# Values, zeros of the order table and gate weights loaded behind the keys and queries of the first quads

## The chip, the cores and the metric

The kernel runs on one NeuronCore of one Trainium2 chip. The metric is device time in microseconds (us). The time before is 711.22 us, the median of three runs.

The engines are named as the profile names them: PE is TensorE's matmuls and PEld its weight loads, DVE is VectorE, ACT is ScalarE, POOL is GpSimd, and SP is SyncE, which here only issues transfers (DMAs). Each engine works through its own instructions in a fixed order; between engines and transfers there are semaphores to wait for. A transfer that SP issues is spread over the core's 16 DMA engines, and the transfers of its queue are served in the order of issue.

## What is computed

```
attention, for 8 batches x 8 heads, 576 tokens, 64 dims, 32 landmarks:
    q_lm, k_lm = means of q and k over groups of 18 tokens
    A = softmax(q k_lm'),  Bm = softmax(q_lm k_lm'),  C = softmax(q_lm k')
    Z = inverse of Bm by 6 Newton steps
    x = A Z C v                                   # 4608 tokens x 512
experts:
    logits = x w_gate;  e = argmax(logits);  gate = softmax(logits)[e]
    out = gate * (relu(x w1[e]) w2[e])            # 8 experts, 512 -> 1024 -> 512
```

All arrays are float32 in HBM. q, k and v are 9.4 MB each.

## The kernel before

**Quads.** The attention works on quads, four heads of one batch: quad i is batch i // 2, heads 0 to 3 or 4 to 7; there are 16. For each quad `load` (line 105) issues one transfer of 576 KB each for keys (`ld_k`), queries (`ld_q`) and values (`ld_v`). They go into a pool with two buffers of each name, so the keys of quad i + 2 wait until quad i's have been read. Below, k0, q0 and v0 stand for keys, queries and values of quad 0, and so on.

**Stages.** `period(i)` (line 408) lets the stages of several quads run side by side. Quad i is in `front`: TensorE transposes its keys and queries head by head (`transposed`, line 112, three transposes of a head into one of two PSUM buffers), ScalarE copies them out, GpSimd (keys, lines 131 to 136) and VectorE (queries, line 125) make the sums for the landmarks. Quad i - 1 is in `middle`: the means (line 141), the products (line 169), and two softmaxes (VectorE's maximum, line 184 to 187; ScalarE's exponential `ce`, line 190). Quad i - 2 is in `values`: transposes of `ce` (line 253), products with the values (line 259), and products with the gate's weights `wg` (line 273). Later stages invert, multiply, and write the tokens to DRAM; from the logits each token's number and gate are scattered into the DRAM table `order` (line 558), which has to hold zeros before.

**Order.** `merge` runs the stages' generators side by side, and a scheduler sets each engine's order from the order and priority in which the code is traced, and from times that it assumes. `period(i)` issues keys and queries of quad i + 1 (for i = 0 also those of quad 0), then the values of quad i - 1. The transfer of `wg` is issued in the constructor of `Attention` (line 98), and the one that writes zeros into `order` (288 KB, line 479) in that of `Routing`, from a tile `zero` that also feeds 14 products that nothing reads (line 478), put there for TensorE's clock.

**Experts.** After the attention the tokens, sorted by expert, go in slots of 128 through the two products of their expert (line 814). This loop has all of its weights and rows in time and is the longest part of the program.

Of the kernel before, what the change touches and what calls it, by code (L numbers as in the profile page):

```python
# [22 lines left out]
M = 32                  # landmarks  # L23
P96, J = 96, 6          # token s = 6 p + j
NT = B * S
DM, NE, DF = 512, 8, 1024
QUAD = 264              # [4 heads x 64 | 8 gate logits]
ITER = 6
BOOST = {0: 0, 1: 0, 2: 0, 3: 200, 5: 200}      # of the stages, by their lag
LAST = 1 << 20  # L30
XG = 4                  # buffers of gathered rows
# [7 lines left out]
def merge(tc, *streams):  # L39
    """Runs generators (generator, units, boost) side by side, each at an even pace; the scheduler prefers the boosted."""  # L40
# [18 lines left out]
class Attention:  # L59
    """Tokens into DRAM, in rows [4, 4, 32]: column (q, c, i) is number 128 c + 32 q + i."""  # L60

    def __init__(self, tc, ctx, front, psum, q, k, v, wg):
# [15 lines left out]
        self.ending, self.pair, self.rows = False, 0, []  # L78
# [7 lines left out]
        e2 = c.tile([128, 2, D], F32, name="e2")            # sums the two halves and takes the mean  # L86
# [11 lines left out]
        nc.sync.dma_start(out=self.wg, in_=wg.rearrange("(h d) e -> d h e", d=D))  # L98
        self.src, self.quads, self.cs, self.ats, self.bs, self.z, self.done, self.fin, self.two = ({} for _ in range(9))

    @staticmethod
    def at_col(j):
        """Where the columns (j % 2, j // 2, p) hold the tokens of j."""
        return 288 * (j % 2) + 96 * (j // 2)

    def load(self, i, names):
        b, g = divmod(i, 2)
        for n in names:
            t = self.src[i, n] = self.ld.tile([P96, 4, J * D], F32, name=f"ld_{n}")
            self.nc.sync.dma_start(out=t, in_=getattr(self, n)[b, 4 * g:4 * g + 4].rearrange("h (p j) d -> p h (j d)", j=J))  # L110

    def transposed(self, i, name):
        """Four heads, [128 (j % 2, d), 4, 288 (j // 2, p)], and their landmarks in both halves [128, 4, 32]."""
# [32 lines left out]
    def front(self, i):  # L146
        """Transposes of quad i; of the last batch also what its inverse needs."""
# [29 lines left out]
    def softmaxes(self, i, outer=None, inner=None):  # L177
        """Of ql . k and ql . kl, without their divisions by the sums."""
# [21 lines left out]
    def middle(self, i):  # L200
        """The softmaxes of quad i."""
# [13 lines left out]
        # softmax over the landmarks of q . kl  # L215
# [23 lines left out]
    def values(self, i):  # L239
        """C v of quad i, and its products with the gate's weights."""  # L240
# [38 lines left out]
    def chain(self, b):  # L279
        """Transposes of the inverses Z of batch b, in blocks.  # L280

        Newton's steps 2 Z - Z B Z from Z = c B' give c B' P, P = (I + R)(I + R^2)...(I + R^32), R = I - c B B'."""
# [6 lines left out]
        bt = self.bk.tile([128, 2, W], F32, name="bt")          # transposed: blocks on the diagonal, and side by side  # L289
# [15 lines left out]
        cc = self.sm.tile([128, 2], F32, name="cc")             # - c  # L305
# [16 lines left out]
        rp = self.bk.tile([128, 2, W], F32, name="rp")          # R^(2^k) in blocks, P  # L322
# [26 lines left out]
    def apply(self, b):  # L349
        """Z C v and Z C v w_gate of batch b, in blocks."""  # L350
# [21 lines left out]
    def final(self, b):  # L372
        """The tokens of batch b."""
# [34 lines left out]
    def period(self, i, nb, extra=()):  # L408
        """One quad's time: quad i is transposed, others are in later stages."""
# [3 lines left out]
        if i + 1 < n:  # L413
            self.load(i + 1, "kq")
        if 0 <= i - 1 < n:
            self.load(i - 1, "v")
# [28 lines left out]
SLOTS = NT // 128 + NE - 1     # at most; NT // 128 at least  # L445
EARLY = 2                       # slots that the most frequent expert of the first CHOOSE batches fills for sure
# [4 lines left out]
class Routing:  # L451
    """The tokens' numbers and gates in DRAM, sorted by expert, NT places for each."""

    def __init__(self, tc, ctx, front, psum, order):
# [19 lines left out]
        # products that nothing reads release TensorE's clock before the first loads arrive  # L474
# [4 lines left out]
        nc.sync.dma_start(out=order.rearrange("(p a) o -> p (a o)", p=128), in_=zero)  # L479
# [552 lines left out]
```

## Time and profile before

| | |
|---|---|
| median of three runs | 711.22 us (709.11 to 712.07) |
| span of the profiled execution | 707.1 us |
| time of the profiled execution outside its span | not given; the median is 4.1 us above the span |
| busy in the span | PE 659.2 us (93%), DVE 521.8 (74%), ACT 400.6 (57%), POOL 343.4 (49%) |
| DMA | 84.70 MB, 120 GB/s on average |

The busy times are averages over stages with different limits. The page divides the span into 40 slices of 17.7 us; one line of it gives the clock that TensorE was granted in each, in tenths. Its two levels are 1.2 and 2.4 GHz, and a slice between 5 and 10 tenths had both. The timelines give each engine's work in order of time, with the idle time before a piece and what ended it in brackets.

### The profile page before, as it was taken

The numbers are of one execution on the slowest core, as the hardware profiler recorded it, in microseconds if no ns is written. First come the engines' busy times: TensorE is split into PE (matmuls) and PEld (weight loads), VectorE is DVE, ScalarE is ACT, GpSimd is POOL, SyncE is SP. The second block draws the span as 40 slices with busy tenths as digits, with TensorE's granted clock in tenths as the row PEclk, the third lists the DMA queues.
The fourth block names the chain that finished last, engine by engine and source line by source line (L and its number), as shares of the span: only waits on it lengthen the run. The fifth ranks groups of instructions, "written<-read, shape, count | busy, mean of one in ns | idle before, by whom it ended". The sixth has DMA issues, their size and how long they took to land.

```text
span 707.1 us, 13813 instructions
## 1 busy us (share of the span) xinstructions
PE 659.2 (93%) x4489; PEld 517.5 (73%) x4489; DVE 521.8 (74%) x1409; ACT 400.6 (57%) x997; POOL 343.4 (49%) x371
## 2 busy tenths in 40 slices
PE   7798989898889869889999999999999999999996
PEld 4576767676667546667888888888888888888884
DVE  2389858579697976657879879876689879857653
ACT  3377656556566563335666666654477576544442
POOL 3355564556447154577654544544445454351231
PEclk8589998978897998999999999999999999999999
DMA  9877676668843171128224514411143333410010
GB/s 201 186 197 176 188 150 167 126 172 177 210 112 98 45 211 35 47 64 300 69 70 142 176 53 160 162 45 57 50 142 110 119 116 112 144 57 35 31 49 29
DMA packets 45386, 84.70 MB, mean 120 GB/s; under 512 B 7954, under 2 KB 26388, under 8 KB 45280
## 3 DMA queue, kind: packets, MB, share of 16 engines
q1 hardware_dynamic: 35232, 63.24, 33.4%
q0 software_dynamic: 10048, 20.29, 9.0%
q8 instruction: 38, 0.62, 0.4%
q14 instruction: 68, 0.56, 0.3%
HBM read 64.29 MB, written 19.73 MB: 119 GB/s over the span
## 4 chain that ended last, share of the span: by engine, by line
PE 46%; DMA 4%; issue 3%; DVE 1%; POOL 1%; ACT 0%; POOLq 0%; DVEq 0%
PE ps_tp L814 12%; PE ps_fi L814 12%; PE ps_ch L814 12%; PE ps_fr L814 11%; DMA xg<-xs,read 4%; DVE h L834 0%; POOL out_dram L845 0%; POOL xg L782 0%; DVE buf L795 0%; DVE ht_lo L800 0%; ACT ht_hi L797 0%; POOLq L880 0%; POOLq L845 0%; DVEq L795 0%; DVEq L771 0%
## 5 line engine op out<-in xcount | busy, mean ns | idle before, releaser
L845 POOL DMA_INDIRECT out_dram<-buf,write x38 | 39.0, 1026 | 166.2 <-ACTq L771 140.6
L782 POOL DMA_INDIRECT xe<-xs,read x84 | 87.7, 1044 | 25.7 <-issue 24.1
L782 POOL DMA_INDIRECT xg<-xs,read x80 | 83.0, 1038 | 30.5 <-issue 23.0
L797 ACT CAST ht_hi<-buf 128x512 fp32r<-128x512 f32 x76 | 47.1, 622 | 71.3 <-DVE buf L795 70.4
L834 DVE TENSOR_SCALAR h<-ps_tp 32x256 f32<-32x256 f32 x152 | 64.1, 422 | 26.9 <-PE ps_tp L814 24.6
L834 DVE TENSOR_SCALAR h<-ps_fi 32x256 f32<-32x256 f32 x144 | 60.7, 422 | 28.5 <-PE ps_fi L814 26.1
L832 ACT ACTIVATE h<-ps_tp 32x256 f32<-32x256 f32 x152 | 57.3, 377 | 41.2 <-PE ps_tp L814 37.4
L832 ACT ACTIVATE h<-ps_fi 32x256 f32<-32x256 f32 x144 | 54.2, 377 | 34.5 <-PE ps_fi L814 30.7
L814 PE MATMUL ps_ch<-whi,ht_hi 128*128 128x512 f32 x152 | 59.7, 393 | 1.0 <-ACTq L771 1.0
L814 PE MATMUL ps_fr<-whi,ht_hi 128*128 128x512 f32 x152 | 60.4, 398 | 0.0
L814 PE MATMUL ps_fr<-wlo,ht_hi 128*128 128x512 f32 x152 | 60.0, 395 | 0.0
L814 PE MATMUL ps_fr<-whi,ht_lo 128*128 128x512 f32 x152 | 59.8, 393 | 0.0
L558 POOL DMA_INDIRECT order<-i_tok,l_at x48 | 44.8, 932 | 30.5 <-issue 9.6
L814 PE MATMUL ps_ch<-wlo,ht_hi 128*128 128x512 f32 x152 | 59.4, 391 | 0.0
L814 PE MATMUL ps_ch<-whi,ht_lo 128*128 128x512 f32 x152 | 59.2, 389 | 0.0
L392 PE MATMUL ps_fi<-w,at 128*96 128x264 f32 x160 | 51.2, 415 | 7.9 <-DVE l L396 5.1
L795 DVE STREAM_TRANSPOSE buf<-h 128x512 f32<-128x512 f32 x76 | 49.7, 692 | 5.8 <-DMA out_dram<-buf,write 2.0
L800 DVE TENSOR_TENSOR ht_lo<-buf,ht_hi 128x512 fp32r<-128x512 f32 x76 | 51.1, 692 | 3.8 <-ACT ht_hi L797 0.2
L759 DVE TENSOR_TENSOR wlo<-raw,whi 128x512 fp32r<-128x512 f32 (+1 forms) x64 | 48.9, 820 | 4.2 <-ACT whi L758 4.1
L814 PE MATMUL ps_tp<-whi,xt_hi 128*128 128x512 f32 x152 | 49.4, 405 | 2.2 <-ACTq L771 2.2
L814 PE MATMUL ps_tp<-whi,xt_lo 128*128 128x512 f32 x152 | 48.5, 401 | 0.0
L814 PE MATMUL ps_tp<-wlo,xt_hi 128*128 128x512 f32 x152 | 48.1, 398 | 0.0
(275 smaller groups left out, 1572.3 us busy)
## 6 DMA issues: line engine op xcount, KB each, us to landing
raw<-in_moe_w_dram SPq DMA_DIRECT2D x48, 512.0 KB, 6.1
ld_k<-in_k_dram SPq DMA_DIRECT2D x16, 576.0 KB, 5.4
ld_q<-in_q_dram SPq DMA_DIRECT2D x16, 576.0 KB, 11.8
ld_v<-in_v_dram SPq DMA_DIRECT2D x16, 576.0 KB, 7.6
xs<-xrow SPq DMA_DIRECT2D x44, 192.0 KB, 4.6
xe<-xs,read POOLq DMA_INDIRECT x84, 2.5
xg<-xs,read POOLq DMA_INDIRECT x80, 3.0
order<-i_tok,l_at POOLq DMA_INDIRECT x48, 6.0
```

Of the source, the lines that this page charges most:

```text
L392: nc.tensor.matmul(po[g][:P96, :QUAD], lhsT=ats[g][:, n:n + 96], rhs=w[:, g, :], start=True, stop=True)
L558: self.nc.gpsimd.indirect_dma_start(out=self.places[n + j], out_offset=bass.IndirectOffsetOnAxis(ap=at[:, j:j + 1], axis=0), in_=self.tok[ ...
L759: (engine or nc.vector).tensor_tensor(out=l, in0=x, in1=h.bitcast(F32), op=ALU.subtract)
L782: self.nc.gpsimd.indirect_dma_start(out=x[:, t, :], out_offset=None, in_=src.rearrange("n (q c) -> (n q) c", q=4), in_offset=bass.Indirect ...
L795: nc.vector.transpose(out=x.rearrange("p c (t j) -> p t c j", t=4), in_=src[:, :, 32 * c:32 * c + 128].rearrange("p t (c i) -> p t c i", c=4))
L797: nc.scalar.copy(out=hi[:, c:c + 4, :], in_=x)
L800: nc.vector.tensor_tensor(out=lo[:, c:c + 4, :], in0=x, in1=hi[:, c:c + 4, :].bitcast(F32), op=ALU.subtract)
L814: nc.tensor.matmul(ps[c // 512] if type(ps) is list else ps[:, c // 512], lhsT=x0[:, a, :], rhs=w[:, a, c:c + 512], start=a == 0 and j == ...
L832: nc.scalar.activation(out=dst, in_=src, func=AF.Relu)
L834: nc.vector.tensor_scalar(out=dst, in0=src, scalar1=0.0, scalar2=None, op0=ALU.max)
L845: nc.gpsimd.indirect_dma_start(out=self.outs[s], out_offset=bass.IndirectOffsetOnAxis(ap=at, axis=0), in_=y, in_offset=None, bounds_check= ...
```

## The change

The loads of `wg` and of the zeros leave the constructors. `wg` is issued in `period(1)`, v0 in `period(1)` and v1 in `period(2)`, each ordered behind the last load of queries issued so far; the zeros are written after `period(2)`, ordered behind v1. Loads of quads 0 and 1 (keys, queries and values) are made as two transfers of two heads each. The tile `zero` and its 14 products stay. (The full diff also strips comments, which moves line numbers.)

```diff
     def load(self, i, names):
         b, g = divmod(i, 2)
         for n in names:
             t = self.src[i, n] = self.ld.tile([P96, 4, J * D], F32, name=f"ld_{n}")
-            self.nc.sync.dma_start(out=t, in_=getattr(self, n)[b, 4 * g:4 * g + 4].rearrange("h (p j) d -> p h (j d)", j=J))
+            m = 2 if i < 2 else 4
+            for h in range(0, 4, m):
+                self.loads[n] = self.nc.sync.dma_start(out=t[:, h:h + m], in_=getattr(self, n)[b, 4 * g + h:4 * g + h + m].rearrange("h (p j) d -> p h (j d)", j=J))
...
         self.wg = c.tile([D, H, NE], F32, name="wg")
-        nc.sync.dma_start(out=self.wg, in_=wg.rearrange("(h d) e -> d h e", d=D))
+        self.gate = wg.rearrange("(h d) e -> d h e", d=D)
...
         if i + 1 < n:
             self.load(i + 1, "kq")
+        if i == 1:
+            with self.tc.issue_after(self.loads["q"].ins):
+                self.nc.sync.dma_start(out=self.wg, in_=self.gate)
         if 0 <= i - 1 < n:
-            self.load(i - 1, "v")
+            with self.tc.issue_after(self.loads['q'].ins) if i < 3 else nullcontext():
+                self.load(i - 1, "v")
...
-        nc.sync.dma_start(out=order.rearrange("(p a) o -> p (a o)", p=128), in_=zero)
+        self.clear = lambda: nc.sync.dma_start(out=order.rearrange("(p a) o -> p (a o)", p=128), in_=zero)
...
                 attention.period(i, B, extra)
+                if i == 2:
+                    with tc.issue_after(attention.loads["v"].ins):
+                        routing.clear()
```

The first place where this shows is the opening of SP's queue. A row is a line of the source, an instruction, what it writes and reads with its shape, and in brackets what it waits for: DMAHW0 to DMAHW7 count the landings of SP's transfers, which take these eight in turn; PE and DVE are those engines' counters. A number behind a name tells buffers apart. Before, from the first transfer on (wg, k0, zeros, q0, k1, q1, v0, v1, k2):

```order
L98 DMA wg_203<-in_moe_w_gate_dram 64x8x8
L110 DMA ld_k_205<-in_k_dram 96x4x384
L479 DMA order_73<-zero_87 128x576 [waits DVE_49]
L110 DMA ld_q_207<-in_q_dram 96x4x384
L110 DMA ld_k_209<-in_k_dram 96x4x384
L110 DMA ld_q_211<-in_q_dram 96x4x384
L110 DMA ld_v_270<-in_v_dram 96x4x384
L110 DMA ld_v_384<-in_v_dram 96x4x384
L110 DMA ld_k_266<-in_k_dram 96x4x384 [waits DMAHW1_49,DMAHW0_49,PE_49]
```

Now (two halves each of k0, q0, k1 and q1, then k2, q2, wg, two halves of v0, k3, q3):

```order
L112 DMA ld_k_203<-in_k_dram 96x2x384 x2
L112 DMA ld_q_206<-in_q_dram 96x2x384 x2
L112 DMA ld_k_209<-in_k_dram 96x2x384 x2
L112 DMA ld_q_212<-in_q_dram 96x2x384 x2
L112 DMA ld_k_268<-in_k_dram 96x4x384 [waits DMAHW1_49,DMAHW0_49,PE_49]
L112 DMA ld_q_270<-in_q_dram 96x4x384 [waits DMAHW3_49,DMAHW2_49,PE_49]
L419 DMA wg_202<-in_moe_w_gate_dram 64x8x8
L112 DMA ld_v_273<-in_v_dram 96x2x384
L112 DMA ld_v_273<-in_v_dram 96x2x384 [waits DMAHW4_49]
L112 DMA ld_k_384<-in_k_dram 96x4x384 [waits DMAHW5_49,PE_49]
L112 DMA ld_q_386<-in_q_dram 96x4x384 [waits DMAHW7_49,DMAHW6_49,PE_49]
```

wg and v0 have moved behind q2, which waits until PE has read q0 out of its buffer.

The second place is what follows on SP's queue now: the halves of v1, the zeros, k4, v2, q4. Before, v1 and the zeros stood in the rows above, and k4, v2 and q4 came right behind q3.

```order
L112 DMA ld_v_388<-in_v_dram 96x2x384
L112 DMA ld_v_388<-in_v_dram 96x2x384 [waits DMAHW0_49]
L485 DMA order_73<-zero_87 128x576 [waits DMAHW1_49,DVE_49]
L112 DMA ld_k_548<-in_k_dram 96x4x384 [waits DMAHW2_49,PE_49]
L112 DMA ld_v_552<-in_v_dram 96x4x384 [waits DMAHW4_49,DMAHW3_49,PE_49]
```

v1 and the zeros now stand between q3 and k4.

The third place is PE around the first products with the values, `ld_v`, in `values` of quad 0: `ce` are the exponentials, `ct` their transposes, `ld_k` here is k2. Before:

```order
L253 MATMUL ps_tp<-ident,ce 96x128 [waits Activation_49]
L253 MATMUL ps_tp<-ident,ce 96x128 x2
L259 MATMUL ps_fr<-ld_v,ct 32x64 [waits DMAHW6_49]
L259 MATMUL ps_fr<-ld_v,ct 32x64 x6
L121 MATMUL ps_tp<-ident,ld_k 128x96 [waits Activation_49]
L121 MATMUL ps_tp<-ident,ld_k 128x96 x2
```

Now:

```order
L255 MATMUL ps_tp<-ident,ce 96x128 [waits Activation_49]
L255 MATMUL ps_tp<-ident,ce 96x128 x2
L261 MATMUL ps_fr<-ld_v,ct 32x64 [waits DMAHW3_49]
L261 MATMUL ps_fr<-ld_v,ct 32x64
L261 MATMUL ps_fr<-ld_v,ct 32x64 [waits DMAHW4_49]
L261 MATMUL ps_fr<-ld_v,ct 32x64 x4
L123 MATMUL ps_tp<-ident,ld_k 128x96 [waits Activation_49]
L123 MATMUL ps_tp<-ident,ld_k 128x96 x2
```

The instructions stand as they stood; the products wait for two landings instead of one, and k2's further heads stand behind them. On PE, DVE, ACT and POOL the whole program is in the same order before and after.

## Rows read from the trace of the kernel before

**Rows 1.** The chain that ended last: start us, us, what.

```profile
318.63 7.37 PE ps_tp L814 x24
...
639.51 5.52 PE ps_fi L814 x24
```

**Rows 2.** The page's slices: TensorE's granted clock in tenths, 17.7 us each.

```profile
PEclk8589998978897998999999999999999999999999
```

**Rows 3.** Timeline of SP's queue: start us, us, queue, line, operation, out<-in.

```profile
0.76 0.75 SPq L98 DMA_DIRECT2D wg<-in_moe_w_gate_dram  x1
...
3.84 1.01 SPq L110 DMA_DIRECT2D ld_q<-in_q_dram  x1
4.89 1.07 SPq L110 DMA_DIRECT2D ld_v<-in_v_dram  x2
8.84 0.31 SPq L110 DMA_DIRECT2D ld_k<-in_k_dram  x1
...
31.47 0.31 SPq L110 DMA_DIRECT2D ld_k<-in_k_dram  x1
```

**Rows 4.** Timeline of PE, opening: [idle before <- what ended it].

```profile
7.11 0.69 PE L121 MATMUL ps_tp<-ident,ld_k 96*128 96x96 f32 x6 [0.24 <-DMA ld_k<-in_k_dram]
...
10.62 0.69 PE L121 MATMUL ps_tp<-ident,ld_q 96*128 96x96 f32 x6 [1.82 <-DMA ld_q<-in_q_dram]
...
13.21 2.42 PE L121 MATMUL ps_tp<-ident,ld_k 96*128 96x96 f32 x12 [0.89 <-DMA ld_k<-in_k_dram]
...
17.35 1.17 PE L121 MATMUL ps_tp<-ident,ld_q 96*128 96x96 f32 x6
...
23.37 0.71 PE L121 MATMUL ps_tp<-ident,ld_k 96*128 96x96 f32 x3 [3.64 <-DMA ld_k<-in_k_dram]
23.87 0.68 PE L141 MATMUL ps_fr<-ls_k,e 128*128 128x128 f32 x2
...
28.88 0.65 PE L259 MATMUL ps_fr<-ld_v,ct 96*32 96x64 f32 x14
...
42.69 0.88 PE L259 MATMUL ps_fr<-ld_v,ct 96*32 96x64 f32 x48
...
44.88 0.41 PE L121 MATMUL ps_tp<-ident,ld_k 96*128 96x96 f32 x3
...
50.73 0.31 PE L259 MATMUL ps_fr<-ld_v,ct 96*32 96x64 f32 x6
...
61.23 0.30 PE L259 MATMUL ps_fr<-ld_v,ct 96*32 96x64 f32 x2
```

**Rows 5.** Windows: stretch, us, busy per engine (instructions); last three: PEclk, DMA share, GB/s.

```profile
2.00:3.00 1.00, 1.00 (x4) 0.40 (x3) 0.83 (x11) 0.04 (x1) 0.13 (x1) 1.00 0.56 46
3.00:4.00 1.00, 1.00 (x4) 0.30 (x2) 0.75 (x6) 0.00 (x0) 0.23 (x1) 1.00 0.87 74
...
20.00:22.00 2.00, 0.00 (x0) 0.00 (x0) 0.86 (x3) 0.00 (x0) 0.00 (x0) 1.00 1.10 238
...
30.00:32.00 2.00, 2.00 (x31) 1.22 (x33) 0.00 (x0) 0.92 (x3) 1.17 (x2) 0.50 0.00 0
...
40.00:60.00 20.00, 18.88 (x304) 14.83 (x303) 16.88 (x54) 15.58 (x50) 11.63 (x15) 1.00 0.73 184
```

**Rows 6.** Waits over the whole span: us in total, times, longest us.

```profile
PE ps_tp L121 <- DMA ld_k<-in_k_dram: 4.8, 3, 3.6
```

**Rows 7.** Tile `ld_k`, first 60 us, from issue to landing where told.

```profile
DMA to landing us min/median/max: 4.6/4.6/4.6
```

**Rows 8.** Timelines of ACT, DVE and POOL before v0's first use.

```profile
24.76 0.75 ACT L190 ACTIVATE ce<-ps_sc,c_mx 128x576 f32<-128x576 f32 x1
...
20.72 0.17 DVE L187 TENSOR_SCALAR c_mx<-c_mx 128x2 f32<-128x2 f32 x1
...
18.79 0.49 POOL L136 TENSOR_TENSOR ls_k<-ls_k,ls_t 128x128 f32<-128x128 f32 x1
```

**Rows 9.** Timeline of POOL: the first scatter into the table `order`.

```profile
90.59 1.12 POOL L558 DMA_INDIRECT order<-i_tok,l_at  x1 [1.11 <-DVE l_at L547]
```

More of the change, by code (lines that the diff above doesn't have):

```diff
@@ L77, in __init__ @@
         self.p_tp, self.p_sc, self.p_fr, self.p_ch, self.p_fi = psum
-        self.ending, self.pair, self.rows = False, 0, []
+        self.ending, self.pair, self.rows, self.loads = False, 0, [], {}
         c = self.const
```

## The prediction

> **What bounds the kernel now.** I read the page's slices first, then the chain that ended last, then the first 62 us in the timelines of SP's queue and of TensorE, then the list of waits. The chain [rows 1] stands on TensorE from 318.63 us to the end of its loop at 645.03 us, in blocks of 24 matmuls of 5.5 us without a gap, and closes with a tail to the end of the span. Nothing in the change reaches that loop; it can only start it earlier or later. So the question is how early the attention stages before it run. There TensorE's clock stands out: 8 and 5 tenths in the first two of the 40 slices, the 5 lower than in any other [rows 2].
>
> The timeline of SP's queue [rows 3] shows that all early loads are issued by 5.96 us, in the order wg, k0, zeros, q0, k1, q1, v0, v1 (k0 is the keys of quad 0), and that k2 follows at 8.84 us. They are served one behind the other: TensorE's waits for loads end at 7.11 (k0), 10.62 (q0), 13.21 (k1) and 23.37 us (k2) [rows 4]. From k1 to k2 four transfers land (q1, v0, v1, k2), so one of 576 KB takes (23.37 - 13.21)/4 = **2.54 us**, and the DMA engines are busy throughout (238 KB in each us of 20 to 22) [rows 5]. TensorE does nothing from 20 to 22 us, then stands at 23.37 with k2. But v0, which landed before k2, is not used until 28.88 us [rows 4], and v1 not until 42.69. The values are in the queue some 6 us and more too early, and the keys behind them too late. That is what the change touches. Later no load is waited for: over the whole span TensorE waits for keys 3 times, 4.8 us in all [rows 6], and those are the waits at 7.11, 13.21 and 23.37.
>
> **The change part by part.** The order tables show that on SP alone the order changes; on TensorE, VectorE, ScalarE and GpSimd every instruction stands where it stood, and only some wait on other transfers. So a gain of X at a point through which everything passes moves all that follows by X, unless a load or the clock takes it back.
>
> *Zeros and wg out of the opening.* The zeros stood between k0 and q0: that step took 10.62 - 7.11 = 3.51 us instead of 2.54, so they cost 0.97 us. wg was first in the queue, 16 KB in pieces of 32 bytes, and in the two us from 2 to 4 the DMA moved 46 and 74 KB [rows 5]. At the steady 232 KB a us these 120 KB take 0.5 us, so between 0 us (if any first transfer starts so slowly) and 1.5 us (if it was wg) comes free; I take 1.0. k0 would land at about 6 us, but TensorE waited only 0.24 us for it, having come from its 14 opening products [rows 4]: k0 itself gains 0.24 us at most. k1 lands at 13.21 - 0.97 - 1.0 = 11.24, q1 at 13.78 us.
>
> *Two transfers for each of k0, q0, k1, q1, v0, v1.* The bytes and their pieces of 1536 bytes stay. A transposition of heads 0 and 1 can start when the first half is there, 1.27 us earlier; this hides in the wait for k2 and v0, which come later, so I count nothing for it. On the other side there are five more transfers ahead of v0's last byte. Issuing one takes SP 0.31 to 1.01 us [rows 3], hidden as long as the queue holds work, and it does: eight issues are done by some 6 us, when the transfers have work until 13.8. What a transfer may cost beside its bytes is bounded by the lone load: 4.6 us from issue to landing [rows 7], which is 2.06 more than 2.54. Queued transfers show none of it, since 2.54 us is the whole step between two landings; I take 0, with 2.06 each as the end of the bound (a rival below).
>
> *k2 and q2 ahead of v0.* k2 is issued once k0 is transposed, in the trace at 8.84 us, long before its turn at 13.78; q2 waits for q0's transposition, which comes with q0 and so again ahead of its turn at 16.32. So k2 lands at 13.78 + 2.54 = **16.32 us** instead of 23.37. From k2 to v0's first use TensorE took 28.88 - 23.37 = 5.51 us, at half clock: the first head of k2, the means of quad 1, the exponentials, the transposes of ce [rows 4, 8]. Do the inputs of that piece come early enough too? GpSimd's sums of k1 ended at 18.79 + 0.49 = 19.28 us, 6.07 after k1 [rows 8]: 17.31 us now, where the means want them at 16.32 + 0.50 = 16.82. That costs 0.49 us. VectorE's maximum of quad 0 ended at 20.89, 3.54 after q1's second half began on TensorE at 17.35: 13.78 + 3.54 = 17.32, where ScalarE's exponential needs it at 16.32 + 1.39 = 17.71. So TensorE is ready for v0 at 16.32 + 5.51 + 0.49 = 22.32 us.
>
> *v0 behind q2 and wg.* This is the wait that is added: TensorE's products with v0 stop its queue, and behind them stand the other heads of k2, all of q2 and quad 1's products. v0 lands at 16.32 + 2.54 (q2) + 1.0 (wg) + 2.54 = **22.40 us**. It is used at 22.40 instead of 28.88: **6.48 us earlier**. The two times, 22.32 and 22.40, lie so close that either bound may decide; with the bounds on wg (0 to 1.5 us at the start, 0.1 to 1.0 in its new place) v0 lands between 21.0 and 23.4.
>
> *v1 and the zeros behind k3 and q3.* SP's new waits are for counters of transfers long ahead in the queue (v1's second half for k2 at 16.32, the zeros for q2 at 18.86 us), so they hold nothing up. The queue goes on with k3 24.94, q3 27.48, v1 30.02, zeros 31.0, k4 33.5, v2 36.1 us. Wanted, at the pace of before: v1 at 42.69 - 6.48 = 36.2, k4 at 44.88 - 6.48 = 38.4 us. k4's issue, at 31.47 before, moves to 25.0, ahead of its turn; the DMA's idle time at 30 to 32 us [rows 5] is filled. The zeros are needed by the first scatter into the table at 90.6 us [rows 9], so they cost nothing there.
>
> *The clock.* It was full (2.4 GHz) from 20 to 22 us, where TensorE did nothing, half of that at 30 to 32, where it never paused, and full from 40 to 60 [rows 5]. So it fell after the stop that ended with k2. In the new order TensorE still has waits before v0, so I let it fall as before and stay down for the same work: no gain, no loss. The sum is **-6.5 us**: the span of the profiled execution would go from 707.1 to 700.6. The time of that execution outside its span isn't given; the median of the runs, 711.22, is 4.1 above the span, and I leave that as it is: 711.22 - 6.48 = **704.7 us**.
>
> **The rivals.** *The clock stays up.* From v0's first use to v1's took 13.81 us at half clock; at full clock the next two such steps took 50.73 - 42.69 = 8.04 and 61.23 - 50.73 = 10.50 us [rows 4], 9.27 on average. If fewer stops of TensorE before 22 us keep the clock up, another 4.5 us comes free: 704.7 - 4.5 = **700.2 us**. v1 would be wanted at 31.7 and k4 at 33.9, against 30.0 and 33.5: the loads just allow it. For it speaks that two long stops shrink (1.82 us at q0, 3.64 at k2); against it, that the work from 16 to 22 us is thin.
>
> *The clock stays down longer.* The rise at 40 us came after 16 us in which TensorE had hardly stopped. If waits for v0 put the rise off by one such step, 4.5 us are lost: **709.2 us**. Beyond 100 us the page shows slices at 7 and 8 [rows 2]; a shift of these against the work can give or take one or two us in any case.
>
> *Each half pays for itself.* This one ends slower. If the five extra transfers ahead of v0 cost 2.06 us each, v0 lands at 22.40 + 10.3 = 32.7 us, 3.8 later than its use before: **715.0 us**. It decides from 1.3 us a transfer on (6.48/5). Against it stand the landings 2.54 us apart. The Trainium skill, "DMA: Bandwidth & Descriptors", section "Rules for kernel authors", advises transfers of 1 MiB and more and one transfer in place of many; its "Anatomy of one DMA" puts a fixed 2.0 us on each (for transfers of GpSimd's queue). By that figure, an estimate from the page, five more would make 10 us and 714.7. The trace doesn't agree for transfers that queue: the fixed part overlaps the one before.
>
> *It does not take.* If the start of the DMA is slow for any first transfer and another wait on the way (GpSimd's sums, the exponentials) runs late by 2 to 3 us, half of the gain goes: about **708 us**.
>
> **How the numbers follow.** Forecast 704.7 (its own spread 702.5 to 707.5): 0.50. Clock up, 700.2: 0.22. Clock down longer, 709.2: 0.12. It doesn't take, 708: 0.11. Each half pays, 715.0: 0.05. About 0.5%, 3.6 us here, can be told from no change: faster is below 707.7, slower above 714.8. Faster: 0.48 + 0.22 + 0.05 + 0.03 = 0.78; slower 0.04; the rest, 0.18, is within. The range leaves out the last rival and the far half of clock down: from 700.2 less half of the spread of the runs of before (709.11 to 712.07) to 709.2: 699.0 to 709.2 us.
>
> **What would show it.** In the profile after: TensorE's wait for k2 ends near 16.3 us; a wait of TensorE for v0 near 22.4 us takes its place; q0 lands some 2 us earlier while the first keys gain 0.2; the DMA has no idle stretch at 30 us; the loop of 5.5 us blocks starts near 312 us. The forecast is wrong if the two halves of a load together take more than 2.54 us, if k2's issue is late, or if the clock from 23 to 40 us is no longer 0.5; the last would show in v1's first use, 36 us by the forecast, 32 by the rival.

## The result, and the profile after

The changed kernel takes **700.35 us** (median of 19 runs) beside 710.74 us for the kernel before on the same chip (19 runs), 10.4 us less by the medians. The ratio is 0.9887, with a 95% interval from 0.9856 to 0.9917, that is 8 us less, between 6 and 10; it leaves out the slow runs of either kernel, those more than 1.5% above its fastest (7 of the 19 before, 3 of the 19 after), and so lies above the ratio of the two medians, 0.9854. The prediction was 704.7 against 711.22 us, a ratio of 0.9908. Range and direction held. The time alone doesn't tell the forecast from its first rival, "the clock stays up" (700.2 us, a ratio of 0.9845): the medians lie at the rival, the ratio nearer to the forecast. The profile does tell them apart: the clock did not fall where the forecast let it fall.

The profiled execution of the changed kernel has a span of 694.9 us (707.1 before). Its slices, the granted clock in tenths, against [rows 2]:

```profile
PEclk9999989789889998999999999999999999999999
```

The first two slices read 9 and 9 where they read 8 and 5. The queue of SP, against [rows 3] (start us, us, queue, line, operation, out<-in; lines from `load` on stand two or more further down than before):

```profile
3.67 1.01 SPq L112 DMA_DIRECT2D ld_q<-in_q_dram  x2
9.18 0.31 SPq L112 DMA_DIRECT2D ld_k<-in_k_dram  x1
11.09 0.31 SPq L112 DMA_DIRECT2D ld_q<-in_q_dram  x1
11.45 0.74 SPq L419 DMA_DIRECT2D wg<-in_moe_w_gate_dram  x1
12.24 1.09 SPq L112 DMA_DIRECT2D ld_v<-in_v_dram  x2
...
18.30 0.36 SPq L485 DMA_DIRECT2D order<-zero  x1
22.56 0.32 SPq L112 DMA_DIRECT2D ld_k<-in_k_dram  x1
```

The eight halves of k0, q0, k1 and q1 are issued by 4.68 us. k2 follows at 9.18, ahead of its turn, then q2, wg and v0; the zeros come at 18.30 us. TensorE's timeline, against [rows 4] (in brackets the idle time before and what ended it):

```profile
1.54 6.10 PE L484 MATMUL ps_ch<-zero 128*128 128x512 bf16 x14 [1.54 <-DVE zero L479]
7.47 0.66 PE L123 MATMUL ps_tp<-ident,ld_k 96*128 96x96 f32 x6
...
9.33 0.77 PE L123 MATMUL ps_tp<-ident,ld_q 96*128 96x96 f32 x6 [0.19 <-ACT T_k L124]
...
15.73 0.44 PE L123 MATMUL ps_tp<-ident,ld_k 96*128 96x96 f32 x3
...
20.07 0.31 PE L261 MATMUL ps_fr<-ld_v,ct 96*32 96x64 f32 x4
20.98 0.41 PE L261 MATMUL ps_fr<-ld_v,ct 96*32 96x64 f32 x10 [0.61 <-DMA ld_v<-in_v_dram]
...
31.82 0.88 PE L261 MATMUL ps_fr<-ld_v,ct 96*32 96x64 f32 x48
```

The three waits for k0, q0 and k1 are gone, and so is the wait of 3.64 us for k2: TensorE comes to it and begins at 15.73 us, without a wait that shows. One wait for a load is left, 0.61 us for the second half of v0. The stretches, against [rows 5] (us, busy per engine with instructions, then granted clock, DMA share, GB/s):

```profile
2.00:3.00 1.00, 1.00 (x4) 0.40 (x3) 0.83 (x11) 0.04 (x1) 0.13 (x1) 1.00 0.88 277
3.00:4.00 1.00, 1.00 (x4) 0.30 (x2) 0.75 (x6) 0.00 (x0) 0.23 (x1) 1.00 1.11 281
...
16.00:17.00 1.00, 0.50 (x5) 0.30 (x2) 0.92 (x3) 0.40 (x1) 0.54 (x2) 1.00 1.26 205
17.00:18.00 1.00, 0.65 (x4) 0.30 (x2) 0.00 (x0) 0.80 (x3) 0.00 (x0) 1.00 1.00 168
...
30.00:32.00 2.00, 2.00 (x47) 1.50 (x49) 1.86 (x6) 1.90 (x6) 1.78 (x2) 1.00 1.08 234
20.00:40.00 20.00, 16.85 (x292) 13.02 (x292) 17.49 (x52) 14.63 (x45) 11.26 (x15) 1.00 1.10 246
```

The DMA moves 558 KB between 2 and 4 us instead of 120, has no idle stretch at 30 us, and TensorE's clock is full (2.4 GHz) all the way from 20 to 40 us. Ahead of 20 us the two kernels differ as well. In the kernel before the clock was at half already from some 13 us on, before its stop for k2: it fell behind the wait for q0 (1.82 us) and within the one for k1 (0.89 us). [rows 4] show it in the durations (six transposes in 1.17 us, against 0.77 in the changed kernel), and this window of the kernel before shows it too:

```profile
14.00:16.00 2.00, 1.99 (x12) 1.66 (x11) 0.00 (x0) 1.49 (x4) 0.00 (x0) 0.50 1.10 232
```

The chain of work that ended last, against [rows 1] (start us, us, what):

```profile
313.24 5.73 PE ps_ch L820 x24
...
627.32 5.52 PE ps_fi L820 x24
```

Its last block of ps_fi starts 12.2 us earlier than in [rows 1] (639.51), which is the whole difference of the two spans. Followed along the way, TensorE is ahead by 23.37 - 15.73 = 7.6 us at k2, 28.88 - 20.07 = 8.8 at v0, 42.69 - 31.82 = **10.9 us** at v1 and 61.23 - 51.15 = 10.1 at v3. So the gain is made in the first 32 us. It isn't carried on unchanged: the lead is 203.64 - 197.21 = 6.4 us at v12 (the values of quad 12), 242.34 - 232.09 = 10.3 at v15 and 12.2 at the end. After 32 us both executions have stretches at half clock, at different places.

### The profile page after: what moved, and what is told of

Its sections match the earlier page's. It is cut to its first block, busy times and chain, and to the rows that moved or that the text cites. A ratio compares the mean times of both kernels' runs of the same rounds, so it can differ in the third digit from the quotient of the medians.

```text
span 694.9 us, 13825 instructions
## 1 busy us (share of the span) xinstructions
PE 648.9 (93%) x4489; PEld 510.0 (73%) x4489; DVE 521.8 (75%) x1409; ACT 400.6 (58%) x997; POOL 342.9 (49%) x371
## 3 DMA queue, kind: packets, MB, share of 16 engines
HBM read 64.29 MB, written 19.73 MB: 121 GB/s over the span
## 4 chain that ended last, share of the span: by engine, by line
PE 46%; DMA 3%; issue 3%; POOL 1%; DVE 1%; ACT 0%; POOLq 0%; DVEq 0%
PE ps_fi L820 12%; PE ps_ch L820 12%; PE ps_fr L820 11%; PE ps_tp L820 11%; DMA xe<-xs,read 3%; DVE h L840 0%; POOL xg L788 0%; POOL out_dram L851 0%; POOL xe L788 0%; DVE buf L801 0%; DVE ht_lo L806 0%; ACT ht_hi L803 0%; POOLq L886 0%; POOLq L851 0%; DVEq L801 0%
## 5 line engine op out<-in xcount | busy, mean ns | idle before, releaser
L788 POOL DMA_INDIRECT xe<-xs,read x84 | 87.4, 1040 | 25.7 <-issue 23.8
L838 ACT ACTIVATE h<-ps_tp 32x256 f32<-32x256 f32 x152 | 57.1, 376 | 41.3 <-PE ps_tp L820 37.5
L394 PE MATMUL ps_fi<-w,at 128*96 128x264 f32 x160 | 52.6, 424 | 9.4 <-DVE l L398 7.7
L564 POOL DMA_INDIRECT order<-i_tok,l_at x48 | 44.8, 934 | 28.8 <-issue 10.9
```

Of the source, the lines that this page charges most:

```text
L394: nc.tensor.matmul(po[g][:P96, :QUAD], lhsT=ats[g][:, n:n + 96], rhs=w[:, g, :], start=True, stop=True)
L564: self.nc.gpsimd.indirect_dma_start(out=self.places[n + j], out_offset=bass.IndirectOffsetOnAxis(ap=at[:, j:j + 1], axis=0), in_=self.tok[ ...
L788: self.nc.gpsimd.indirect_dma_start(out=x[:, t, :], out_offset=None, in_=src.rearrange("n (q c) -> (n q) c", q=4), in_offset=bass.Indirect ...
L838: nc.scalar.activation(out=dst, in_=src, func=AF.Relu)
```

## The experiments

Two theories were set against each other. **Landings:** the gain is that k2 and v0 land earlier, and every us of that goes through. **Clock:** a good part of it is that TensorE, no longer stopped for loads, keeps its full clock through 20 to 40 us. A third, the rival of the prediction that each transfer pays for itself, was tried beside them. The experiments ran on other chips, on which the kernel before takes 747 to 751 us, so they are read by their ratio to it there and by the opening of their profiles. "k2", "v0" and "v1" below are the times at which TensorE begins with that tile. A profile shows one execution, and the executions of one kernel differ in their clock.

**One transfer for each load.** The changed order with whole loads:

```diff
-            m = 2 if i < 2 else 4
+            m = 4
```

> The changed kernel with whole loads: 576 KB in one transfer each, order of the queue as in the changed kernel. Theory: the halves hide nothing that ends last, k2 and v0 land within 0.3 us of the changed kernel's (15.6 and 20.9 us), the start of the expert loop within 1 us, ratio 0.987 to 0.991. Rival 'halves carry it': q0's and k1's transposes start over 1 us later, TensorE has stops again before 13 us, the clock falls there as before, and over a third of the gain goes: ratio 0.993 or more.

Ratio 0.9892 [0.9847, 0.9938], like the changed kernel's 0.9887. TensorE's timeline of this kernel:

```profile
15.66 0.44 PE L123 MATMUL ps_tp<-ident,ld_k 96*128 96x96 f32 x3
...
21.02 0.42 PE L261 MATMUL ps_fr<-ld_v,ct 96*32 96x64 f32 x14 [0.97 <-DMA ld_v<-in_v_dram]
...
31.88 0.88 PE L261 MATMUL ps_fr<-ld_v,ct 96*32 96x64 f32 x48
```

k2, the end of v0's wait and v1 stand within 0.1 us of where the halves put them. The wait for v0 is longer by 0.36 us, since TensorE cannot begin with the first half at 20.07, but the second half lands when the whole does. Splitting the loads gains nothing here.

**Halves alone.** The kernel before, its order kept, with two transfers for each of the first loads:

```diff
-            self.nc.sync.dma_start(out=t, in_=getattr(self, n)[b, 4 * g:4 * g + 4].rearrange("h (p j) d -> p h (j d)", j=J))
+            m = 2 if i < 2 else 4
+            for h in range(0, 4, m):
+                self.nc.sync.dma_start(out=t[:, h:h + m], in_=getattr(self, n)[b, 4 * g + h:4 * g + h + m].rearrange("h (p j) d -> p h (j d)", j=J))
```

> The kernel before with two transfers for each load of quads 0 and 1 and nothing else: order of the queue as before. Theory: nothing, since k2 and v0 land as before within 0.5 us and the stop before k2 stays: v0's use near 28.5, v1's near 42.5 us, ratio 0.998 to 1.002. Rival 'each half pays': five more transfers ahead of k2 at 2.06 us each, k2 at 33 us, ratio above 1.01. Rival 'halves carry it' (transposes start on half a load, TensorE stops less before 13 us, the clock stays up): v1's use 3 us earlier or more, ratio 0.995 or less.

Ratio 0.9993 [0.9946, 1.0040]: no difference. k2 starts at 21.74 us beside 22.52 in the kernel before on that chip, so six more transfers did not delay it. The opening runs at half clock as in the kernel before on that chip (0.53 from 20 to 40 us), and v1 starts at 41.31 us.

**Four transfers for each load.** The changed kernel with quarters:

```diff
-            m = 2 if i < 2 else 4
+            m = 1 if i < 2 else 4
```

> The changed kernel with every load of quads 0 and 1 in four transfers of one head, so 10 more transfers ahead of v0's last byte. Theory (queued transfers overlap their fixed part): v0's last byte lands within 0.5 us of 20.9, ratio 0.987 to 0.991. Rival 'each transfer pays for itself' at 2.06 us each: v0 lands 20 us later, near 41 us, ratio above 1.01; at 0.5 us each 5 us later, ratio 0.995. A third way: issuing 16 transfers at 0.5 us each takes SP some 8 us, close to the 13 us that their bytes take; if issue were the limit, landings would step by more than 0.64 us a quarter.

Ratio 0.9967 [0.9931, 1.0003]: by the middle values two thirds of the gain are gone, against the theory's 0.987 to 0.991. TensorE's timeline and the window of 20 to 40 us of this kernel:

```profile
15.66 0.44 PE L123 MATMUL ps_tp<-ident,ld_k 96*128 96x96 f32 x3 [1.13 <-DMA ld_k<-in_k_dram]
...
20.23 0.43 PE L261 MATMUL ps_fr<-ld_v,ct 96*32 96x64 f32 x6
21.80 0.44 PE L261 MATMUL ps_fr<-ld_v,ct 96*32 96x64 f32 x8 [1.14 <-DMA ld_v<-in_v_dram]
22.85 0.64 PE L261 MATMUL ps_fr<-ld_v,ct 96*32 96x64 f32 x10
...
36.48 0.88 PE L261 MATMUL ps_fr<-ld_v,ct 96*32 96x64 f32 x48
```

```profile
20.00:40.00 20.00, 18.52 (x247) 14.36 (x245) 12.78 (x42) 10.96 (x32) 10.00 (x13) 0.61 0.88 216
```

k2 starts where it does with whole loads, and the last of v0 is there 0.8 us later; yet v1 starts 4.6 us later (36.48 against 31.88), at a clock of 0.61. Fifteen more transfers ahead of v0's last byte cost (21.80 - 21.02)/15 = 0.05 us each, nowhere near the 2.06 us of the rival. TensorE stops twice for 1.1 us, and the clock falls between the two stops, at 18.4 us: ten products with v0 then take 0.64 us instead of 0.41. So the second stop is not what brought it down. And this execution was the longest of its kernel (754.42 us; the other eleven took 739.41 to 750.34), so the 4.6 us are what such a fall costs, and not what the quarters cost each time.

**Quarters, with the stops filled.** The same, with 14 products that nothing reads, copies of the opening ones, in TensorE's stretches of few instructions:

```diff
-            m = 2 if i < 2 else 4
+            m = 1 if i < 2 else 4
...
+    fill(nc, (("ld_k", 24, 5), ("ls_k", 1, 2), ("ld_v", 3, 5), ("T_q", 8, 2)))
```

(Five ahead of k2's first transpose, two ahead of the means of its sums, five ahead of v0's second part, two ahead of a group of products in quad 1.)

> The kernel with four transfers a load (which lost about 0.7% against whole loads, with the clock at half from 18.4 to 35.4 us in its profile) with 14 more products that nothing reads: 5 ahead of k2's first transpose, 2 ahead of quad 1's means, 5 ahead of the products with v0's last quarter, 2 ahead of quad 1's products. Every other instruction stands where it stood. Theory: what quarters lost is the clock alone; v0's last quarter lands near 21.8 us as before, the clock stays up, v1's use comes near 32.5 us instead of 36.5, ratio to before 0.987 to 0.992. Rival 'more transfers cost by themselves': v1's use 35 us or later, ratio 0.995 or more.

Ratio 0.9932 [0.9897, 0.9967], a little short of the theory's 0.987 to 0.992. Its window and its v1:

```profile
20.00:40.00 20.00, 17.88 (x294) 13.07 (x288) 16.95 (x51) 14.15 (x43) 11.12 (x14) 1.00 1.09 243
```

```profile
32.62 0.88 PE L263 MATMUL ps_fr<-ld_v,ct 96*32 96x64 f32 x48
```

With the same loads in the same pieces the clock is back at 1.00 and v1 at 32.62: 3.9 us earlier than in the quarters without the filling. k2 and v0 start no earlier than there (16.46 and 20.44 against 15.66 and 20.23), so between these two executions it is the clock and not a landing. That the filling brought it about in each execution isn't shown: the two ran on different chips, the one without it was its kernel's longest, and the intervals of the two ratios overlap. The ratios only point the same way.

**The filling in the kernel before.** No load is moved; ten such products stand ahead of k2's first transpose, in the wait of 3.6 us:

```diff
+    at = [n for n, (k, i, t) in enumerate(pe) if "ld_k" in t and "Matmult" in t][24]
...
+    for n in range(FILL):
+        for i in pair:
+            new.append(copy.replace(i, name=f"I-{900000 + len(new)}"))
+    at = pe[at][0]
+    body[at:at] = new
```

> The kernel before with its queue untouched; only 10 more of the products that nothing reads stand on TensorE ahead of k2's first transpose, in the stop from 19.7 to 23.4 us (2.2 us of them at full clock, 4.3 at half). Every other instruction stands where it stood. Theory 'landings and clock': k2 and v0 land as before (23.2 and 18.2 us), but the clock doesn't fall at 23 us; v0's first use near 27.5 (28.9 before), v1's near 37.5 (42.7 before), ratio to before 0.993 to 0.996. Rival 'landings alone': v1's use within 1 us of the time before, ratio 0.999 to 1.001.

Ratio 0.9929 [0.9891, 0.9967]. Two windows of its profile:

```profile
24.00:26.00 2.00, 1.72 (x24) 1.10 (x24) 0.34 (x2) 1.80 (x8) 0.00 (x0) 0.90 1.11 250
26.00:28.00 2.00, 2.00 (x34) 0.87 (x18) 1.24 (x3) 0.79 (x3) 0.00 (x0) 0.50 1.09 248
```

The clock is at half from 12 us, as in the kernel before, and full from some 18.8 us, just ahead of the filling; it stays full as far as 25.6 us, through the rest of the stop. Then it falls for 3.4 us, and again from about 36 to 39 us; over 20 to 40 us it is 0.83, against 0.50 in the kernel before profiled again. v1 starts at 40.36 us instead of 42.29; the theory had 37.5. So the clock alone, with every load where it was, gives 2 us at v1. The ratio says some 5 us (0.0071 of 750; the medians, 747.25 and 750.37, say 3), and this profile doesn't show where the other 3 lie; the median granted clock of its runs is 0.922 against 0.9165 beside it, so full clock later in the kernel is likely, but that is not shown.

**The kernel before, profiled again**, unchanged, for the opening on this chip:

> The kernel before once more, for a second profile of it beside the others of this call. If the stop before k2 is what brings TensorE's clock down: half clock again from about 23 to 40 us, v0's first use near 28.9 and v1's near 42.7 us. If the half clock of the first profile was an accident of that execution: full clock in that stretch and v1's use near 38 us.

One run, 751.18 us. k2 starts at 22.52 after a wait of 3.19 us, v0 at 28.04, v1 at 42.29, all but the last 2 us at a clock of 0.50:

```profile
10.00:20.00 10.00, 7.99 (x64) 6.46 (x64) 4.04 (x9) 5.13 (x14) 5.12 (x8) 0.64 1.09 241
...
24.00:26.00 2.00, 1.93 (x8) 1.55 (x8) 0.33 (x2) 1.46 (x7) 0.00 (x0) 0.50 1.11 245
```

The half clock was no accident of one execution. But in this one it wasn't the stop before k2 that brought it down: it stands at half from some 13 us (0.64 over 10 to 20 us) to 40 us, through that stop.

From k2 to v1 it takes 19.8 us (19.3 in the profile ahead of the prediction). With a full clock that step takes 14.5 to 16.2 us in six kernels (the changed one 16.1, whole loads 16.2, and 14.5 in the one below that moves only the values, where TensorE waits for no load on this way), and 17.5 to 18.2 in three where the clock fell and rose again in between. In the kernel below that moves only wg and the zeros it takes 15.6 us, with the first 5 of them at half clock. So waits that a faster TensorE runs into take back a part of what the clock gives.

**The two halves of the move, apart.** Only wg and the zeros go behind; values stay where they were:

```diff
-            m = 2 if i < 2 else 4
+            m = 4
...
-            with self.tc.issue_after(self.loads['q'].ins) if i < 3 else nullcontext():
-                self.load(i - 1, "v")
+            self.load(i - 1, "v")
...
-                    with tc.issue_after(attention.loads["v"].ins):
+                    with tc.issue_after(attention.loads["q"].ins):
```

> The gate weights and the zeros alone leave the opening; v0 and v1 stay ahead of k2, and every load is one transfer. Theory 'landings and clock' (the gain comes from k2 and v0 landing earlier and from TensorE's clock that stays up because the stop before k2 is gone): k2 lands near 20.7 us (23.2 before, 15.6 with the whole change), v0's first use near 26.2 (28.9 and 20.1); the stop before k2 is still 4 to 5 us long, so the clock still falls, and only 2.5 to 3 us are gained: ratio to before 0.996. Rival 'opening alone' (what counts is the slow start of the first transfers, the rest is hidden): most of the gain is here already, ratio 0.990 or less.

Ratio 0.9969 [0.9936, 1.0001]. TensorE still stops for k2 and its clock is at half there, from some 11 to 25 us, of which this is a part:

```profile
19.76 0.71 PE L123 MATMUL ps_tp<-ident,ld_k 96*128 96x96 f32 x3 [3.11 <-DMA ld_k<-in_k_dram]
```

```profile
16.00:20.00 4.00, 0.89 (x26) 0.52 (x10) 1.35 (x4) 0.00 (x0) 0.15 (x1) 0.50 1.10 253
```

k2 comes 2.8 us earlier than in the kernel before on the other chip, v1 6.9 us earlier (35.35). The theory let the clock stay down behind this stop; it rose 5 us after k2, where in the kernel before, behind a stop as long (3.19 us), it rose after 17.6 us. How long the clock stays down after k2 is thus not settled by the stop alone. And only the values go behind (not all of the diff is shown; the two issues in `period` and behind it go as well):

```diff
-        self.gate = wg.rearrange("(h d) e -> d h e", d=D)
+        nc.sync.dma_start(out=self.wg, in_=wg.rearrange("(h d) e -> d h e", d=D))
...
-            m = 2 if i < 2 else 4
+            m = 4
...
-        self.clear = lambda: nc.sync.dma_start(out=order.rearrange("(p a) o -> p (a o)", p=128), in_=zero)
+        nc.sync.dma_start(out=order.rearrange("(p a) o -> p (a o)", p=128), in_=zero)
```

> The values alone move (v0 behind q2, v1 behind q3); gate weights and zeros stay in the opening, loads are whole. Theory 'landings and clock': k2 lands near 18.2 us, v0 near 23.3, its first use there; TensorE's stop before k2 is gone, so the clock stays up from about 20 us on, and v1's first use comes near 34 us (42.7 before, 31.8 with the whole change): ratio 0.989 to 0.991. Rival 'landings alone' (the clock is as low as before, or does not matter): v0's use 5.5 us earlier and v1's also 5.5 us earlier, at 37.2: ratio 0.992 to 0.993.

Ratio 0.9959 [0.9928, 0.9990]; k2 at 18.39, without a wait, v0 at 22.46, v1 at 32.87 us, clock 0.66 from 10 to 20 us and 1.00 from 20 to 40. For the values alone both theories had expected more (0.989 to 0.993). The two gains, 0.0031 and 0.0041, add up to 0.0072; both parts together, with whole loads, gave 0.0108. With these intervals that is no proof of more than a sum. In the profiles only both together keep the clock full from 10 to 40 us.

**Without the opening products.** The changed kernel, 13 of the 14 products ahead of k0 left out (nothing reads them):

```diff
+    drop = [k for k, i in enumerate(body) if i.engine == mybir.EngineType.PE and "zero" in i.concise()][2:]
+    for k in reversed(drop):
+        del body[k]
```

> The changed kernel without 13 of the 14 opening products; every other instruction stands where it stood. k0's transposes start when k0 lands, near 4.0 us instead of 7.5, at half clock. Theory 'landings and clock': k2 (15.6) and v0 (20.9) land as with the change, so the early start is worth nothing at v0's use; the clock comes up only some time between 12 and 33 us; if after 23, v1's use is 2 to 4.5 us later than the 31.8 of the changed kernel: ratio to before 0.990 to 0.995. Rival 'the opening products are in the way' (k0 lies ready for 2 to 3 us behind them, and this counts): v1's use 2 us earlier than 31.8, ratio 0.986 or less.

Ratio 0.9892 [0.9853, 0.9930], no difference to the changed kernel. TensorE's timeline of it:

```profile
4.06 2.43 PE L123 MATMUL ps_tp<-ident,ld_k 96*128 96x96 f32 x12 [1.91 <-DMA ld_k<-in_k_dram]
...
12.79 1.17 PE L123 MATMUL ps_tp<-ident,ld_q 96*128 96x96 f32 x6
...
15.33 0.72 PE L171 MATMUL ps_sc<-T_k,lm_q 64*32 64x288 f32 x16
...
16.03 0.47 PE L123 MATMUL ps_tp<-ident,ld_k 96*128 96x96 f32 x3
```

k0 starts at 4.06 us instead of 7.47, so in the changed kernel it is the opening products, and not the load, that hold k0 up. But its transposes run at half speed (six in 1.17 us, where they take 0.77 and less at full clock), the clock rises by 15.3 us, and k2 starts at 16.03 instead of 15.73. What the products give in clock they take in time.

**v0 ahead of q2.** A version meant to do away with the last wait:

```diff
-            self.load(i + 1, "kq")
+            self.load(i + 1, "kq" if i != 1 else "k")
+            if i == 1:
+                with self.tc.issue_after(self.loads['k'].ins):
+                    self.load(0, "v")
+                with self.tc.issue_after(self.loads['v'].ins):
+                    self.load(2, "q")
```

> The changed kernel with v0's two halves ahead of q2 (queue: k2, v0, q2, wg, k3). v0's last byte lands near 18.1 us instead of 20.9, q2's near 20.8 instead of 18.2, where it is used at 23.6. Theory: the added wait of TensorE for v0 (0.61 us in the changed kernel's trace, for the second half) goes, nothing else takes its place; v0's products and what follows come 0.6 to 0.9 us earlier; ratio to before as the change's less 0.001: 0.986 to 0.990. Rival: q2 becomes the wait and gives it back: v1's use at 31.8 or later.

Ratio 0.9897 [0.9854, 0.9939], no better. Its timeline and its window:

```profile
19.12 0.42 PE L261 MATMUL ps_fr<-ld_v,ct 96*32 96x64 f32 x14
...
25.94 0.73 PE L171 MATMUL ps_sc<-T_q,lm_k 64*32 64x288 f32 x7 [1.00 <-issue]
...
33.55 0.88 PE L261 MATMUL ps_fr<-ld_v,ct 96*32 96x64 f32 x48
```

```profile
20.00:40.00 20.00, 17.57 (x258) 13.82 (x255) 14.74 (x48) 12.95 (x41) 11.05 (x14) 0.83 1.08 244
```

v0 is used 1 us earlier and without a wait, and q2 isn't waited for either. TensorE stops for 1.0 us until 25.94, for nothing that the profile shows ("issue"), the clock is at half from 25.7 to 32.5 us, and v1 is 1.7 us later than in the profile of the changed kernel. The rival's 31.8 or later came, but not by its wait for q2; whether the new order has a part in that stop is open.

**The changed kernel again**, in the same comparison:

> The changed kernel once more, for a second profile beside the others of this call. Theory: v0's first use near 20.1 us and v1's near 32 us as in its first profile, with the clock up from the opening to some 55 us; ratio to before 0.986 to 0.992. If its clock was luck in the first profile: a stretch at half clock between 15 and 35 us and v1's use at 33.5 to 36.5 us.

Ratio 0.9898 [0.9863, 0.9933]. Its opening is not the one shown above:

```profile
21.14 0.41 PE L261 MATMUL ps_fr<-ld_v,ct 96*32 96x64 f32 x10 [1.15 <-DMA ld_v<-in_v_dram]
...
33.12 0.88 PE L261 MATMUL ps_fr<-ld_v,ct 96*32 96x64 f32 x48
```

```profile
24.00:26.00 2.00, 2.00 (x19) 1.70 (x12) 1.97 (x5) 1.37 (x4) 1.76 (x4) 0.50 1.09 240
```

The wait for v0 is twice as long here, and the clock is at half from 23.4 to 30.2 us, which puts v1 1.3 us later. So the full clock is what the new order makes possible, not what it makes sure of.

**The changed kernel with its thin stretch filled**, ten products in four places:

```diff
+    fill(nc, (("ld_k", 24, 2), ("ls_k", 1, 2), ("ld_v", 2, 3), ("T_q", 8, 3)))
```

> The changed kernel with 10 more of the products that nothing reads (0.22 us each at full clock), set in the thin stretch: 2 ahead of k2's first transpose, 2 ahead of quad 1's means, 3 ahead of the products with v0's second half, 3 ahead of quad 1's products at 26 us. Every other instruction stands where it stood. If the clock sometimes falls in the thin stretch of the changed kernel and costs 4 us then, this keeps it up in all executions: ratio to before 0.003 below that of the changed kernel in this call, and a smaller spread. If the clock stays up there anyway: the same ratio within 0.001.

Ratio 0.9895 [0.9854, 0.9936]. The clock stays at 1.00 and v1 starts at 31.38 us, 0.4 earlier than in the first profile of the changed kernel and 1.7 earlier than in the second. In the time of the whole it can't be told from the changed kernel, and its profiled execution, with the earliest v1 of all, was the longest of its six (746.47 us). No version tried beats the changed kernel.

## Why the prediction came out as it did

**What held.** The gain is made in the opening, and the later loads stay in time: v1 and k4 are not waited for, and the zeros delay nothing. That a gain moves all that follows by as much, unless the clock takes it back, needed its condition: the lead swings between 6.4 and 12.2 us after v1. The halves are worth nothing, as counted (0.9892 whole, 0.9887 and 0.9898 in halves, 0.9993 alone). The rival in which each transfer pays 2.06 us is out: 0.05 us was measured.

**The start of the queue.** I took 1.0 us for wg at the start, with 1.5 as the upper end. [rows 5] show 120 KB from 2 to 4 us, the profile after 558: the 438 KB between them are 1.9 us at 232 KB a us, but the kernel before makes up a part of them from 6 to 8 us (334 KB a us against 241). The landing of k2 gives the cost: it came 7.64 us earlier, of which v0 and v1 are 2 x 2.54 and the zeros 0.97, so 1.6 are left for wg. The upper end was nearer. Whole loads without wg ahead show nearly the same (147 and 339 KB in these two us), and the halves with wg ahead do not (36 and 171), so the slow start belongs to wg, not to any first transfer.

**wg in its new place.** Taken at 1.0 us, from the same row. The stretch in which it is served moves 205 and 168 KB where 232 are usual: (27 + 64)/232 = 0.4 us. A small transfer in 32-byte pieces cost less between two large ones here than at the head of the queue. Both terms together put k2 and v0 earlier: v0's last half is used at 20.98 and not at 22.40 us, and k2, forecast to be waited for until 16.32, is begun at 15.73 us.

**k0.** It was to gain 0.24 us at most, and it lost 0.36: k0 was there, but the opening products took 6.10 us instead of 5.34 and ended at 7.6. This cost nothing, since k2 decides the opening and not k0.

**From k1 to k2.** The sum took k2's landing alone for its start and left out TensorE's own way there. At half clock that way takes 6.3 to 6.5 us (from k1 at 13.21 to 19.73, which is k2's start less its idle 3.64, in [rows 4]; from 10.38 to 16.65 with only wg and the zeros moved). From the forecast's k1 at 11.24 it would have ended near 17.6 us and not at 16.32, and v0 would have come near 17.6 + 5.5 = 23.1 and not at 22.40. So the forecast, by its own clock, gave some 0.7 us too much. It didn't show, because the clock was full: the way took 4.3 us, and TensorE came to k2 at about its landing (in the second profile of the changed kernel it waited 0.51 us for it, until 15.54).

**From k2 to v0.** The step of 5.51 us at half clock, with 0.49 for the sums, gave 22.32. It took 20.07 - 15.73 = 4.34 us. The wait for the sums came as foreseen (0.50), one of 0.25 for the exponentials came with it, and the work between them ran at full clock.

**The clock.** This is the step that failed: "I let it fall as before". Its reading of before was incomplete too: there the clock was at half from 13 us on, not only after the stop that ended with k2. From k2 to v1 the kernel before took 19.32 us and the changed one 16.09; the difference, **3.2 us** of the 10.9 at v1, is what the clock gives there, net of the waits that come up at the faster pace. The remaining 7.6 is k2's landing, which TensorE could use in full only at full clock: at half it would have come to k2 near 17.6 us, so by this estimate some 2 us of the 7.6 hang on the clock as well. The forecast had 6.5 at v0 and v1, with nothing for the clock. That the clock has a part of its own is shown by the filling in the kernel before, with no load moved (40.36 against 42.29 at v1, ratio 0.9929); the quarters, with and without filling (36.48 and 32.62), point the same way in one execution each. How the whole gain divides between landing and clock in the average run is not shown. The rival had the mechanism but not quite its size or place: it let the gain fall between v0 and v1 with a step of 9.27 us. That step took 11.75, with 0.61 us of waiting for v0 and 0.98 for ScalarE's `be` in it, and 1.2 of the clock's 3.2 us fall ahead of v0 (5.51 against 4.34). That its 31.7 us for v1 fits so well (31.82 measured) is luck in part, since its errors cancel: v0's first use 2.3 us too late (22.40 against 20.07), the step 2.5 too short.

**The chance.** I gave the full clock 0.22, with the thin work from 16 to 22 us against it. That doubt had something: in the second profile of the changed kernel the clock did fall, at 23.4 us. (The lower end of the range is a slip: 700.2 less half of the spread is 698.7, not 699.0.)

**What stays open.** In the profiles the spans differ by 12.2 us and the openings by 10.9, while the interval of the ratio ends at 10. An execution's opening doesn't give its time. The second profile of the changed kernel is 9.2 us ahead of the kernel before on its chip at v1, 4.0 at v15 and 5.8 at the end. With only the values moved v1 comes 9.4 us earlier than in the kernel before, and the ratio says 3 us; with only wg and the zeros it is 6.9 and 2.3. Later stretches at half clock fall differently in each execution; how much of the opening's gain they give back on average was not measured.

## What to carry to other kernels

Order the loads at the start by first use, not by when they can be issued: two loads of values that were used 10 us and more after they had landed (v0 two steps of 2.54 us ahead of k2, so near 18.3, and used at 28.88) held up the keys behind them by 5.1 us, and the zeros and the gate weights by another 2.6. When a stop of TensorE goes away, work out the stretch behind it at both clock levels before you choose one, since here the clock was worth 3.2 us behind the landing beside the 7.6 of the landing itself, and TensorE had to be at full clock to be at k2 when it landed. Check a forecast at v1 against the time of the whole: here the openings and the ratios of the parts did not agree. Splitting a queued load gained nothing here, where its last part was waited for.

## What the runs showed of the hardware

- TensorE's clock can stand at half while TensorE has no pause: from 24 to 26 us of the second profile of the changed kernel it was busy for 2.00 of 2.00 us at 0.50. The falls in the openings came with or after stops for a load or for another engine: 1.15 us for v0 there; in the kernel before 1.82 for q0 and 0.89 for k1 (it fell at 12.7 us, within the second), and 3.64 for k2 (it fell at 23.0 us). Products that nothing reads, put into such stops, were followed by full clock to 40 us in two kernels and to 25.6 us in a third. After a stop of some 3.1 us at half clock it rose 5 us after k2 in one kernel and 17.6 us after it in another.
- A queued transfer of 576 KB cost the same in one, two or four pieces, to 0.05 us a piece ((21.80 - 21.02)/15).
- 16 KB in pieces of 32 bytes cost some 1.6 us at the head of the queue (7.64 us that k2 came earlier, less 5.08 for two loads and 0.97 for the zeros), and 0.4 us between large transfers (205 and 168 KB a us instead of 232).
- Ahead of some 15 us the row of the granted clock can read 1.00 while the matmuls run at half: without the opening products it reads 1.00 from 10 to 20 us, and six transposes take 1.17 us. Where the row and the durations differ, the durations tell.
